# A second feed-forward layer whose down projection is done in the seven-product form

## The chip, the cores and the metric

The kernel runs on one core of a Trainium2 chip. The metric is the device time of one execution in microseconds, from the first to the last instruction with what lies around it. A profiled execution gives a trace as well; times in the trace count from its first instruction.

## The reference

Two layers, each a Fourier mixing and a gated feed-forward, on x of 2048 rows (S) and 640 columns (D); the feed-forward is F = 1728 wide.

```python
def _A_ref(x, dft_seq_re, dft_seq_im, dft_hid_re, dft_hid_im):
    a = jnp.einsum("bsd,ed->bse", x, dft_hid_re)
    b = jnp.einsum("bsd,ed->bse", x, dft_hid_im)
    return jnp.einsum("ts,bse->bte", dft_seq_re, a) - jnp.einsum("ts,bse->bte", dft_seq_im, b)

def _B_ref(x, w_gate, w_up, w_down):
    g = jnp.einsum("bsd,df->bsf", x, w_gate)
    u = jnp.einsum("bsd,df->bsf", x, w_up)
    return jnp.einsum("bsf,fd->bsd", _sigmoid(g) * u, w_down)

for _ in range(2):
    x = x + _A_ref(_layernorm(x), ...)
    x = x + _B_ref(_layernorm(x), B_w_gate, B_w_up, B_w_down)
```

The result is fp32 of the size of x.

## The kernel before

**Numbers.** Each fp32 operand is kept as two fp16 parts, a high part and what it leaves (HI, LO). A product of two such operands takes three matmuls, high by high, high by low and low by high (`PASSES`, line 134). Scales are powers of two (`DS` for w_down, `PH` for the hidden activations).

**Fourier part.** `folded` uses the symmetries of the DFT matrices, so that a quarter of the products is left (`sequence`, `hidden`, lines 773 and 855). That the matrices given have these symmetries, and that the weights lie within the scales, is tested on the chip while the layers run: `load_rows`/`test_rows`, `load_cols`/`test_cols` (lines 1293 to 1319), `load_hidden_rows`, `load_hidden_cols`, `test_w`, `load_edges`. A DFT test loads four pieces of 128 KB through GpSimd's queue (POOL) into one of two rooms, takes differences of mirrored pieces on VectorE (DVE), and adds up their squares on ScalarE (ACT, `square_rest`, line 1277). If the tests fail, the program runs `general` afterwards, a plain version of the whole.

**Feed-forward.** The rows are worked on in four blocks of 512 (`NB`, b = 0 to 3), with the hidden width in tiles of 128: 13 full ones (j = 0 to 12) and a half one, j = 13 (`NF` = 13). Block 0 computes gate and up directly (`gate_up`, line 1051). Blocks 1 to 3 do it by seven products in place of eight for each tile j, in steps of two tiles (`seven`, line 1174, which calls `part_one` to `part_seven`, all through `products`, line 1097). The weights of such a step are G (320 KB), S (512 KB, sums of gate and up weights) and U (192 KB), loaded by `load_s` on SyncE's queue (SP) some steps ahead. The rows of the block, transposed and with their own sums, stand in `XW`, of which there are two, used in turn by `b % 2`; `pair_apply`, `pair_combine`, `pair_parts` make them during the down of the block before, and `pair_transpose` writes them with transposing DMAs (line 516). `up_parts` splits the result h, 512 tokens wide, into two fp16 parts: `ht`, one slot for each j.

**Down.** For each block and each of its four tiles of 128 rows, `down` (line 1235) accumulates over all j in two PSUM banks, one for each half of the 640 columns (`EH` = 320), 82 matmuls (line 1244) in two steps of 42 and 40, and adds the result into X (line 1259); in layer 2 `store_x` writes the rows out at once. The split w_down (`w`, 2, j) lies in a fixed region and is read again from DRAM for layer 2 (`load_w_again`).

**Order.** The kernel writes the order of every engine's queue by hand. `steps` lists TensorE's work; `at(u, f, ...)` puts a piece of other work before step u, and fractions of u order the pieces within a step (a step of `seven` counts two and has four places for pieces, `some(0)` to `some(3)`). So each engine gets its instructions in the order of these places, and each runs its queue in order, waiting on semaphores where data or a slot are not ready. `block[b]` is the first step of block b, `d0` the first of a down.

**Memory.** All tiles lie in `big`, in units of 128 fp32 columns. X, the two `XW` and the split w_down have fixed places; the rest is shared out by `Slots.take` in program order, and a tile that gets a slot waits for the last readers of what was in it. The eight PSUM banks are handed out in the order in which they were freed (`bank`, `free_bank`).

## Time and profile before

| what | value |
|---|---|
| time, median of 3 runs | 1161.23 us (1159.2 to 1161.76) |
| time of the profiled execution | 1158.61 us |
| its span | 1156.8 us |
| granted TensorE clock | 0.999 |
| DMA, mean | 187 GB/s, 216.46 MB |

The page gives each engine's busy time and its share of the span, forty slices of the span with the busy tenths of each engine, and the chain of work that ended last, followed back from the last instruction. PE is TensorE's matmuls, PEld its weight loads. In a row of a group stand line, engine, operation, output and input with shapes and count; then busy time, mean length of one in ns, and the idle time of the engine in front of them with what ended it. In a row of windows stand the stretch and its length, then busy time and count of each engine, the granted clock, the DMA share and GB/s.

### The profile page before, as it was taken

How to read it: one execution, taken by the hardware profiler on the slowest of the kernel's cores; microseconds unless marked ns; L12 is line 12 of the kernel's file. 1: busy time of each engine (PE TensorE's matmuls, PEld its weight loads, DVE VectorE, ACT ScalarE, POOL GpSimd, SP SyncE). 2: the span in 40 equal slices, each digit the busy share in tenths (PEclk: the TensorE clock that was granted, in tenths of full speed). 3: DMA queues.
4: the chain of work that ended last, by engine and by line, in shares of the span. 5: the costliest groups of instructions: out<-in, count | busy, mean ns of one | idle time of the engine just before them, and what ended most of it. 6: DMA issues, size and time to landing. Idle time of an engine off the chain costs nothing.

```text
span 1156.8 us, 22767 instructions
## 1 busy us (share of the span) xinstructions
PE 1127.3 (97%) x8784; PEld 860.0 (74%) x8784; DVE 738.5 (64%) x1636; ACT 507.7 (44%) x1094; POOL 368.4 (32%) x581
## 2 busy tenths in 40 slices
PE   6699999999999999999999999999999999999997
PEld 2467446788878887888776844678887888788875
DVE  7996888768747676585428567666974457524540
ACT  6864575155525653365304322325552455225420
POOL 2312675223545454421000023453355223221000
PEclk9999999999999999999999999999999999999999
DMA  8417698967495959878103562698649881996301
GB/s 267 148 46 236 241 355 281 259 209 212 144 265 182 252 179 194 264 191 258 47 18 110 190 200 73 129 264 262 222 142 258 247 270 56 199 240 184 132 19 38
DMA packets 158693, 216.46 MB, mean 187 GB/s; under 512 B 70194, under 2 KB 103883, under 8 KB 158574
## 3 DMA queue, kind: packets, MB, share of 16 engines
q1 hardware_dynamic: 140014, 166.97, 49.8%
q0 software_dynamic: 18560, 47.93, 14.1%
q8 instruction: 71, 1.16, 0.4%
q14 instruction: 48, 0.39, 0.1%
HBM read 171.03 MB, written 30.40 MB: 174 GB/s over the span
## 4 chain that ended last, share of the span: by engine, by line
PE 84%; DMA 2%; ACT 1%; POOL 1%; DVE 0%; issue 0%; SPq 0%; DVEq 0%; POOLq 0%
PE acc L1097 40%; PE acc L1244 31%; PE acc L1051 8%; PE acc L855 2%; PE acc L1180 2%; PE acc L773 1%; DMA kept_s<-big 1%; DMA kept_w<-big 1%; ACT big L236 1%; DVE big L238 0%; POOL big L1001 0%; PE acc L523 0%; ACT big L479 0%; ACT big L480 0%; POOL big L999 0%
## 5 line engine op out<-in xcount | busy, mean ns | idle before, releaser
L1097 PE MATMUL acc<-big 128*128 128x256 f16 x4212 | 462.8, 273 | 0.0
L1097 PEld LDWEIGHTS <-big 128*128 128x128 f16 x4212 | 412.1, 98 | 48.2
L1244 PE MATMUL acc<-big 128*128 128x320 f16 x2624 | 357.7, 299 | 0.0
L1244 PEld LDWEIGHTS <-big 128*128 128x128 f16 x2624 | 256.7, 98 | 99.7
L1293 POOL DMA_DIRECT2D big<-in_ct x256 | 175.1, 689 | 232.5 <-DVE big L1302 108.0
L1101 ACT ACTIVATE big<-acc 128x256 f32<-128x256 f32 x312 | 116.1, 381 | 208.9 <-PE acc L1097 207.5
L1051 PE MATMUL acc<-big 128*128 128x512 f16 (+1 forms) x990 | 176.5, 340 | 0.8 <-ACT big L236 0.5
L1051 PEld LDWEIGHTS <-big 128*128 128x128 f16 x990 | 96.5, 98 | 79.8 <-ACT big L236 1.0
L1277 ACT ACTIVATE big<-big 128x768 f32<-128x768 f32 (+8 forms) x104 | 79.4, 764 | 112.5 <-DVE big L1302 80.4
L1165 DVE TENSOR_TENSOR big<-big 128x512 f16<-128x512 f32 x78 | 53.8, 689 | 108.9 <-ACT big L1164 108.9
L1259 DVE SCALAR_TENSOR_TENSOR big<-acc,big 128x320 f32<-128x320 f32 x64 | 28.4, 484 | 91.6 <-PE acc L1244 91.5
L238 DVE SCALAR_TENSOR_TENSOR big<-big 128x640 f16<-128x640 f32 (+6 forms) x81 | 64.4, 833 | 2.9 <-ACT big L236 2.3
L1143 ACT ACTIVATE big<-big 128x512 f32<-128x512 f32 x78 | 47.9, 627 | 41.4 <-DVE big L1134 41.2
L236 ACT ACTIVATE big<-big 128x640 f16<-128x640 f32 (+7 forms) x81 | 50.7, 665 | 16.6 <-POOL big L1001 5.3
L1310 POOL DMA_DIRECT2D big<-in_ct x40 | 27.3, 686 | 94.9 <-ACT big L1277 47.3
L1134 DVE TENSOR_TENSOR big<-big,acc 128x512 f32<-128x512 f32 x78 | 53.1, 681 | 3.3 <-PE acc L1097 3.1
L1164 ACT ACTIVATE big<-big 128x512 f16<-128x512 f32 x78 | 48.8, 626 | 7.1 <-DVE big L1155 6.3
L1153 DVE SCALAR_TENSOR_TENSOR big<-acc,big 128x256 f32<-128x256 f32 x78 | 32.6, 418 | 27.9 <-PE acc L1097 22.4
L1299 DVE TENSOR_TENSOR big<-big 128x256 f32<-128x256 f32 x64 | 26.6, 416 | 36.8 <-DMA big<-in_ct 36.8
L855 PE MATMUL acc<-big 128*128 128x321 f16 (+3 forms) x324 | 48.8, 300 | 1.0 <-DVE big L238 1.0
L1300 DVE TENSOR_TENSOR big<-big 128x256 f32<-128x256 f32 x64 | 26.9, 421 | 30.9 <-DMA big<-in_ct 30.9
L509 ACT ACTIVATE big<-big 128x384 f16<-128x384 f32 (+2 forms) x48 | 28.9, 647 | 37.6 <-DVE big L491 17.9
(186 smaller groups left out, 1055.0 us busy)
## 6 DMA issues: line engine op xcount, KB each, us to landing
big<-kept_w SPq DMA_DIRECT2D x125, 320.0 KB, 6.7
big<-kept_s SPq DMA_DIRECT2D x75, 512.0 KB, 5.5
big<-in_ct POOLq DMA_DIRECT2D x256, 128.0 KB, 4.7
big<-kept_w SPq DMA_DIRECT2D x78, 192.0 KB, 5.5
kept_w<-big SPq DMA_DIRECT2D x41, 320.0 KB, 5.3
big<-in_ct POOLq DMA_DIRECT2D x32, 256.0 KB, 3.9
kept_s<-big SPq DMA_DIRECT2D x13, 512.0 KB, 5.2
big<-in_wg SPq DMA_DIRECT2D x16, 320.0 KB, 3.2
```

Source lines behind the costliest of these rows:

```text
L236: nc.scalar.activation(dh, src, AF.Copy, scale=s)
L238: nc.vector.scalar_tensor_tensor(dl, src, s, dh, op0=OP.mult, op1=OP.subtract)
L855: nc.tensor.matmul(ps[:m, :EC], z[:, at : at + m], w[:, 384 * wp : 384 * wp + EC], start=(d == 0 and zp == HI and wp == HI), stop=(d == ND ...
L1051: nc.tensor.matmul(ps, w[wp][:, d * P : (d + 1) * P], xt[:, xp, :], start=(d == 0 and wp == HI and xp == HI), stop=(d == ND - 1 and wp == LO))
L1097: nc.tensor.matmul(ps, wt, xt, start=start and n == 0, stop=n == len(todo) - 1, skip_group_check=not start)
L1101: nc.scalar.activation(dst, ps, AF.Copy)
L1134: nc.vector.tensor_tensor(v, v, other, op=OP.add)
L1164: nc.scalar.activation(s.parts[HI], v, AF.Copy)
L1165: nc.vector.tensor_tensor(s.parts[LO], v, s.parts[HI], op=OP.subtract)
L1244: nc.tensor.matmul(held["pd", e][0][:, :EH], held["ht", j].parts[hp][:, i * P : (i + 1) * P], held["w", 2, j].parts[wp][:, e * EH : (e + 1 ...
L1277: nc.scalar.activation(v, v, AF.Square, accum_out=new_sum()[:p])
L1293: nc.gpsimd.dma_start(v[:, g], bass.AP(ct.tensor, (r * S + row) * S, [[P, NS], [d * S, 16], [1, P]]))
```

## The change

In layer 2 the down of each block takes tiles 0 to 11 in six pairs (`NP` = 6, `PAIRED`). For a pair p let A11, A21 be the first and second 256 tokens of tile 2p of h, A12, A22 those of tile 2p+1, and B11, B12, B21, B22 the column halves of the two tiles of w_down. Then

```
S1 = A21 + A22    T1 = B12 - B11    P1 = A11 B11   P5 = S1 T1
S2 = S1 - A11     T2 = B22 - T1     P2 = A12 B21   P6 = S2 T2
S3 = A11 - A21    T3 = B22 - B12    P3 = S4 B22    P7 = S3 T3
S4 = A12 - S2     T4 = B21 - T2     P4 = A22 T4
C11 = P1 + P2     C12 = P1 + P6 + P5 + P3
C21 = P1 + P6 + P7 + P4             C22 = P1 + P6 + P7 + P5
```

Each product runs over the six pairs for two tiles of 128 rows (i = 0, 1). Products 1, 6, 7 and 8 share chain a, in which the sum grows and is read after each of them; 5 and 3 share chain b; 2 has c, 4 has d: eight banks. "Product 8" is only the rest, tiles 12 and 13, which also goes along with 2, 3 and 4.

```diff
-DS = 2.0**11
+DS = 2.0**9
-PH = 2.0**-16
+PH = 2.0**-18
+NP = 6
+PAIRED = (), (0, 1, 2, 3)
...
+    def first_parts(p, v):
+        a = both(take(6, "A", p, top=UNITS - 8 * NP), 768)[:, :, :256]
+        f = take(8, "af", p).f32
+        nc.vector.tensor_tensor(f[:, 512:768], v[:, :256], v[:, 256:], op=OP.subtract)
+        nc.scalar.activation(a[:, 0], v[:, :256], AF.Copy)
+        nc.vector.tensor_tensor(a[:, 1], v[:, :256], a[:, 0], op=OP.subtract)
+
+    def second_parts(p, v, w):
+        a, f = both(held["A", p], 768)[:, :, 256:], held["af", p].f32
+        s1, s2, s4 = (f[:, 256 * n : 256 * (n + 1)] for n in (0, 1, 3))
+        nc.scalar.activation(a[:, 0], w, AF.Copy)
+        nc.vector.tensor_tensor(s1, v[:, 256:], w[:, 256:], op=OP.add)
+        nc.vector.tensor_tensor(s2, s1, v[:, :256], op=OP.subtract)
+        nc.vector.tensor_tensor(s4, w[:, :256], s2, op=OP.subtract)
+        nc.vector.tensor_tensor(a[:, 1], w, a[:, 0], op=OP.subtract)
+
+    def sum_parts(p):
+        f, s = held["af", p].f32, both(take(8, "AS", p, top=UNITS), 1024)
+        for c in (slice(0, 512), slice(512, 1024)):
+            nc.scalar.activation(s[:, 0, c], f[:, c], AF.Copy)
+        for c in (slice(0, 512), slice(512, 1024)):
+            nc.vector.tensor_tensor(s[:, 1, c], f[:, c], s[:, 0, c], op=OP.subtract)
+        drop("af", p)
...
+    def make_t(p):
+        v, w = (held["dr", 2 * p + k].f32 for k in range(2))
+        b11, b12, b21, b22 = v[:, :EH], v[:, EH:], w[:, :EH], w[:, EH:]
+        nc.vector.tensor_tensor(b11, b12, b11, op=OP.subtract)
+        nc.vector.tensor_tensor(b12, b22, b12, op=OP.subtract)
+        nc.vector.tensor_tensor(b22, b22, b11, op=OP.subtract)
+        nc.vector.tensor_tensor(b21, b21, b22, op=OP.subtract)
...
+        def mm():
+            for n, i in todo:
+                first = (CHAIN[n], i) not in held
+                if first:
+                    held[CHAIN[n], i] = bank()
...
+                for m, (a, w) in enumerate(mms):
+                    nc.tensor.matmul(held[CHAIN[n], i][0][:, :EH], a, w, start=first and m == 0, stop=m == len(mms) - 1,
+                                     skip_group_check=not first)
...
+        def post():
+            for n, i in todo:
...
+                nc.vector.scalar_tensor_tensor(xe, ps[:, :EH], CB, xe, op0=OP.mult, op1=OP.add)
...
+                    order = [[(n, 0), (n, 1)] for n in (1, 5, 2, 3, 6, 4, 7, 8)]
+                else:
+                    order = [[(n, 0), (n, 1)] for n in (1, 5)] + [[(m, i), (n, i)] for i in range(2) for m, n in ((6, 2), (7, 3), (4, 8))]
+                steps += [down_pairs(b, todo, not first) for todo in order]
...
-                u = block[b] - 8 + 1.2 * i
+                u = block[b] - 8 + (0.4 + 2.2 * i if b - 1 in PAIRED[layer] else 1.2 * i)
...
+                    elif q[0] == 0 and j > 3 and b in PAIRED[layer]:
+                        k = j % 2
+                        for what, v in (("G", u - 2 - 0.5 * k), ("S", u - (0.5 if j == NF - 1 else 1 + 0.5 * k)), ("U", u - k)):
+                            at(v, load_s, j, what)
...
-            u0, u1 = block[0] + 8, block[2] + 14
+            free = (block[0] + 4, block[0] + 13, 10), (block[1] + 1, block[1] + 13, 14), (block[2] + 1, block[2] + 13, 14)
```

What else it moves, in words:

- `gated_parts` and `up_parts` call `first_parts` for an even tile and `second_parts` for an odd one; `sum_parts(p)` follows at the end of the step after. The parts of a pair take 6 + 8 units (`A`, `AS`) where two `ht` took 4 + 4, and 8 more (`af`) while they are made.
- The combinations T1 to T4 are made from the raw w_down once, in layer 1's last down (`load_raw`, `make_t`, `split_t`, `keep_t`, a pair every 1.1 steps), and kept in DRAM. T1 lies where B12 lay in the w_down region (`load_down_again`); T2 and T3, 983 KB each, are loaded in layer 2's block 0 into the place of the second `XW` and stay; T4 is loaded for each block by POOL's queue 2.6 steps into its down, and in block 3 into X's first rows.
- From layer 2's block 0 on there is one `XW` (`place`), so the rows of the next block are written when the last gate product of this one has read it. Their preparation starts 0.4 and 2.6 steps into the down instead of 0 and 1.2, and G, S, U of the next block's tiles 0 to 3 are loaded 4, 3, 1 and 0.5 steps ahead of it instead of 8, 7.9, 4.5 and 3.5.
- G and U share one slot of 8 units. In layer 2's blocks 1 to 3, from tile 4 on, S is loaded 1 to 1.5 steps ahead instead of 2 to 2.5, and U at the start of the step that uses it.
- `store_x` of blocks 0 to 2 comes in the next block's gates (`store_later`).
- Tests: layer 1 takes four more of the DFT tests; in layer 2 the DFT tests stand only in the gates, 10 in block 0 and 14 each in blocks 1 and 2, none in the downs; the test of the gate weights moves from block 0 to block 3 (`test_g`); B12's is done in one piece (`test_others`). The combine, join and add of the Fourier rows q = 2 and q = 3 move to block 0's gates. The last `wh` loads go by POOL's queue instead of SP's.
- The row `fw` of layer 1 is spilled to DRAM and read back.

304 lines of the change are left out of this document (258 added, 46 removed).

## The prediction

> **What bounds the kernel now.** First the page's totals, its slices and its chain.
>
> ```profile
> span 1156.8 us, 22767 instructions
> ...
> PE 1127.3 (97%) x8784; PEld 860.0 (74%) x8784; DVE 738.5 (64%) x1636; ACT 507.7 (44%) x1094; POOL 368.4 (32%) x581
> ...
> PE   6699999999999999999999999999999999999997
> ...
> DVE  7996888768747676585428567666974457524540
> ...
> PE 84%; DMA 2%; ACT 1%; POOL 1%; DVE 0%; issue 0%; SPq 0%; DVEq 0%; POOLq 0%
> ```
>
> From the seventh slice on TensorE is never free, and the chain is its matmuls. Removing matmuls there shortens the end one for one, until something else is late. The same chain in order of time, layer 2's last part:
>
> ```profile
> 730.38 44.55 PE acc L1244 x328
> 774.94 71.39 PE acc L1097 x654
> ...
> 1105.82 44.57 PE acc L1244 x328
> 1150.39 0.02 issue
> 1150.41 0.49 DVE big L1259
> ```
>
> A block's down is 328 matmuls in 44.55 us, and nothing stands between it and the next block's gates. What each layer-2 stage has to spare is in the windows (length; then PE, PEld, DVE, ACT, POOL busy; clock, DMA share):
>
> ```profile
> 563.82:608.37 44.55, 44.55 (x330) 32.09 (x329) 10.77 (x31) 1.70 (x3) 1.26 (x1) 1.00 0.06 19
> 649.18:730.38 81.20, 81.20 (x438) 42.65 (x437) 53.18 (x102) 20.03 (x39) 22.94 (x42) 1.00 0.41 127
> 774.94:855.50 80.56, 80.56 (x740) 72.18 (x739) 63.17 (x148) 43.89 (x101) 39.84 (x67) 1.00 0.68 210
> 855.50:900.05 44.55, 44.55 (x330) 32.12 (x329) 24.61 (x58) 13.44 (x26) 20.48 (x29) 1.00 0.91 248
> 900.05:980.62 80.57, 80.57 (x741) 72.19 (x739) 49.08 (x122) 42.41 (x99) 21.68 (x40) 1.00 0.57 187
> 1025.17:1105.82 80.65, 80.65 (x741) 72.19 (x739) 37.98 (x77) 39.00 (x101) 8.09 (x7) 1.00 0.57 165
> ```
>
> They are layer 1's last down, then block 0's gates, block 1's gates and down, and the gates of blocks 2 and 3. VectorE has 17 to 43 us free in a gate stage; DMA has little left in a down.
>
> **The change part by part.** *Matmuls removed.*
>
> ```profile
> L1097 PE MATMUL acc<-big 128*128 128x256 f16 x4212 | 462.8, 273 | 0.0
> L1244 PE MATMUL acc<-big 128*128 128x320 f16 x2624 | 357.7, 299 | 0.0
> ```
>
> An old down has 4 x 2 x (13 x 3 + 2) = 328 matmuls. The new one has seven products x 2 row tiles x 6 pairs x 3 = 252, and the unpaired tiles 12 and 13 take 4 x 2 x (3 + 2) = 40: 292. Four blocks lose 4 x 36 = 144, each 357.7 / 2624 = 0.136 us at the same 320 columns: **-19.6 us**. A gate matmul is 462.8 / 4212 = 0.110 us; I use both to place things.
>
> *VectorE's added work.* For a pair of tiles the combinations replace two 512-wide subtractions (L1165) by five instructions of 256 columns and three of 512: five 256s and one 512 more. What they cost back to back, the timeline of VectorE shows:
>
> ```profile
> 842.03 0.42 DVE L1299 TENSOR_TENSOR big<-big 128x256 f32<-128x256 f32 x1
> 842.36 0.42 DVE L1300 TENSOR_TENSOR big<-big 128x256 f32<-128x256 f32 x1
> 842.82 0.49 DVE L1302 TENSOR_TENSOR big<-big 128x128 f32<-128x128 f32 x2
> 843.23 0.68 DVE L1165 TENSOR_TENSOR big<-big 128x512 f16<-128x512 f32 x1
> 843.83 0.81 DVE L229 TENSOR_REDUCE wmax<-big 128x1 f32<-128x640 f16 x1
> 844.56 0.41 DVE L1133 TENSOR_TENSOR big<-big 128x256 f32<-128x256 f32 x1
> ```
>
> Start to start, 256 columns take 0.33 us, 512 take 0.60, a weight test 0.73, one DFT test 1.20. So a pair adds 5 x 0.33 + 0.60 = 2.25, a block 13.5; by the full lengths (0.42, 0.68) it is 2.8 and 16.7, and I take the first, since in a full queue the next instruction starts before the last has ended. Block 1 also loses the ten combine, join and add instructions of q=3 to block 0, some 6 us by width, and keeps about the same number of DFT tests: 63.2 + 13.5 - 6 = 71 of 80.6. Block 0 gets those of q=2 and q=3 (12), four DFT tests more (4.8) and 13 weight tests fewer (-9.5): 53.2 + 13.5 + 12 + 4.8 - 9.5 = 74 of 81.2. Blocks 2 and 3 come to about 65 and 61. All fit. ScalarE gets one 256 and one 512 more a pair, at most 0.381 + 0.626 = 1.0 us by these rows, 6 a block, on 44 at most of 80.6:
>
> ```profile
> L1101 ACT ACTIVATE big<-acc 128x256 f32<-128x256 f32 x312 | 116.1, 381 | 208.9 <-PE acc L1097 207.5
> ...
> L1164 ACT ACTIVATE big<-big 128x512 f16<-128x512 f32 x78 | 48.8, 626 | 7.1 <-DVE big L1155 6.3
> ```
>
> [...]
>
> *How late VectorE runs.* Adding up what each step of two tiles gives it (10.6 us usual in 11.7 us of PE; row statistics of the next block add 2.1 each at steps 8 and 10, and a third test falls into step 8), VectorE ends step 10 of block 1 five to six us behind. The chain banks that a step writes are freed by the `up` of the step before, some 6 us ahead of need: 0 us if that sum holds, 2 if it is short by two. I take 0.5. In the down VectorE then stands before `pair_combine` of the second half, whose slot the first half's transposes still read. Behind it wait the reads of products 2 and 3; product 5's read, which product 3 needs, is ahead of it.
>
> *Loads with less lead.* The paired tiles hold 14 units each, so weight slots get tight: `load_s` now waits for a slot that `up_parts` or `up` of the step before has just left. Example: S of tile 5. Its slot is free 0.2 us into the step, and its first use (part_six) stands 45 matmuls in, 45 x 0.110 = 5.0: lead 4.8. Going so through the changed kernel's order, these have under 7 us: block 1, S5 4.8, S7 5.3, G11 5.0, G12 5.3; block 2, S5 4.8, S7 5.3, G9 6.2, G11 6.2, G12 4.9; block 3, S5 6.2, S9 4.7, S11 4.7, S12 6.8. Landing times of S (L1024), of single 320 KB loads (L978) and of G with S and U right behind it (L1022):
>
> ```profile
> L1024 SPq DMA_DIRECT2D big<-kept_s x75: 319/383/2047, 222.7 to 1083.3; - x75
> ...
> DMA to landing us min/median/max: 4.0/5.5/14.8
> ```
>
> ```profile
> L978 SPq DMA_DIRECT2D big<-kept_w x47: 319/382/1166, 279.0 to 1086.0; - x47
> ...
> DMA to landing us min/median/max: 3.8/5.2/6.9
> ```
>
> ```profile
> L1022 SPq DMA_DIRECT2D big<-kept_w x78: 319/544/2126, 215.1 to 1082.9; - x78
> ...
> DMA to landing us min/median/max: 3.2/8.0/13.3
> ```
>
> At the shortest landings nothing waits: 0. At 5.5 for S and 5.2 for G, which now goes out alone as in L978, the shortfalls are 0.7 + 0.2 + 0.2, then 0.7 + 0.2 + 0.3, then 0.8 + 0.8: **+3.9**, which I take. At 8.0 for all thirteen they sum to 34. SP's queue is in order: while an S waits for its slot, U of the same step and the next G stand behind it; U has over 8 us.
>
> *One place for the rows (XW).* The transposes now wait for the block's last gate product and are issued later; behind them on SP's queue stand G, S and U of the next block's first tiles, formerly ahead.
>
> ```profile
> 865.66 6.10 SPq L516 DMA_TRANSPOSE big<-big  x2
> ...
> 875.72 6.95 SPq L516 DMA_TRANSPOSE big<-big  x2
> 882.72 1.57 SPq L1022 DMA_DIRECT2D big<-kept_w  x1
> ```
>
> Now the second pair is issued 20.2 us after the down's start. In the changed kernel the first pair goes out at 13.5 (VectorE is late), its slot is released by about 21, the second pair is ready at 25 and through SP at 32; G lands at 37 to 40, and the down lasts 292 x 0.136 = 39.8. 0 to 3 us at the starts of blocks 2 and 3; block 1's, where VectorE is not late, is safe. I take 0.5 each: +1. T4 (983 KB through POOL) has a lead of 13.7 us in a full DMA stage: 0 to 2 each in blocks 1 and 2, I take 0.5 in all.
>
> *Chain a.* Product 8 of row tile 1 overwrites what L1259's successor must first read; product 8 of tile 0 (5 x 0.136 = 0.68) covers its 0.48:
>
> ```profile
> L1259 DVE SCALAR_TENSOR_TENSOR big<-acc,big 128x320 f32<-128x320 f32 x64 | 28.4, 484 | 91.6 <-PE acc L1244 91.5
> ```
>
> 0 to 0.4 a block; 0.1 each, +0.4. Twice as many such reads (16 a block) lie in downs that have lost their tests.
>
> *At nothing:* the combinations of W2 in layer 1's last down, 24 subtractions of 320 columns and 12 low parts of 640, by the spacings above about 0.40 and 0.73 each, 18 us of VectorE, and 12 high parts, some 9 of ScalarE; the first window covers them (10.8 and 1.7 busy of 44.55, DMA 0.06). Without that cover the first folds after the down would be late. T2 and T3, loaded once, go into block 0's gates (DMA 0.41). Stores move from downs into gates (0.91 to 0.57). Four tests more in layer 1, the spilled row, the last wh loads on POOL's queue: each a few us on engines with room.
>
> **Sum:** -19.6 + 0.5 + 3.9 + 1 + 0.5 + 0.4 = -13.3. The profiled execution took 1158.61 (span 1156.8), so 1145.3; its time stands 2.6 below the median of the runs, 1161.23, which becomes **1148**.
>
> **The rivals.** *Nothing waits.* All terms but the first vanish: 1161.2 - 19.6 = 1141.6. For it: shortest landings. Against: thirteen loads below 7 us of lead. 14%.
>
> *The weight loads set the pace (slower).* Place: the slots of S and G, blocks 1 to 3. At 8.0 us a load the waits are 34 in place of 3.9: 1178. It turns the change into a loss where the landings average above some 6.7 us (17 us of waits). For it: L1022's median, DMA share 0.68 in block 1's gates, stores added there. Against: the 8.0 is of trains of 1 MB. 8%.
>
> *VectorE becomes the bound.* Its waits in block 1's gates:
>
> ```profile
> DVE big L1165 <- ACT big L1164: 8.4, 8, 2.1
> DVE big L1300 <- DMA big<-in_ct: 5.9, 4, 4.3
> ```
>
> If the three splits of a pair each wait 1.05 (8.4 / 8) for ScalarE, 18.9 a block, and these waits stay, block 1 needs 71 + 3 + 18.9 + 14.3 = 107, 27 too many, 21 after the 6 that are free; block 2, in the same way, 14, block 3 some 5: +40, 1187. Against: when VectorE is late, ScalarE is ahead of it. [...] 7%. That the program's own test falls over the changed scale (DS) and the general path runs: 1%.
>
> **How the numbers follow.** Forecast 70%, its own range 1143 to 1157. 0.2% is 2.3 us, about what a measurement of this kernel can tell from no change: faster ends at 1158.9. Faster: 0.68 + 0.14 = 0.82; the forecast's upper end and milder forms of the two slow rivals give 0.05 for same; slower 0.13. The range takes in the free case and stretches up to where the loads eat the gain: 1141 to 1162.
>
> **What would show it.** The down group at 292 matmuls a block in layer 2 and 39.8 us long; gaps in TensorE only in front of S and G products, most in block 1, none in block 0, each below 2 us; VectorE about 71 us busy in block 1's gates. It is wrong if TensorE idles over 8 us in all, if it waits for VectorE's reads of PSUM, or if a down starts late.

## The result, and the profile after

| what | before | after |
|---|---|---|
| time, median of 4 runs each | 1161.49 us (1159.2 to 1165.15) | 1193.18 us (1186.93 to 1197.6) |
| profiled execution, its span | 1158.61 us, 1156.8 | 1197.6 us, 1195.8 |
| granted TensorE clock | 0.999 | 0.986 |

The ratio is 1.0265, with an interval of 1.023 to 1.03: slower by 32 us, where 13 us less were forecast. The traced execution of the changed kernel is the slowest of its four, so stages read from the traces differ by 39 us in all (the spans). The page of the changed kernel has these totals, slices (forty of some 30 us; the clock in tenths), shares of the chain, and the groups of the gates' and the downs' matmuls:

```profile
span 1195.8 us, 22910 instructions
...
PE 1119.2 (94%) x8640; PEld 847.9 (71%) x8640; DVE 829.9 (69%) x1849; ACT 531.9 (44%) x1154; POOL 378.7 (32%) x594
...
PE   5699989999999999999999999998899999849997
...
L1177 PE MATMUL acc<-big 128*128 128x256 f16 x4212 | 473.7, 275 | 37.5 <-ACT big L1181 17.8
...
L1460 PE MATMUL acc<-big 128*128 128x320 f16 x1168 | 159.9, 299 | 5.2 <-DVE big L1477 3.7
```

The 144 matmuls are gone (8784 to 8640) and TensorE is busy 8 us less, yet the gates' products (L1177, formerly L1097) stood still for 37.5 us in front of them, where it was 0.0. The same 4212 products also took 473.7 us in place of 462.8. Of these 10.9 us, some 8 come from products run at a granted clock of 0.50 (the last section shows the stretches); the rest stands at full clock in stages that are interrupted often (block 1's gates: 83.33 busy, less some 1.5 for their stretch at 0.50, against 80.56 before). The chain of waits in order of time shows layer 2's block 0 as it was meant (gates, then down):

```profile
661.39 81.20 PE acc L1122 x435
742.59 39.73 PE acc L1460 x292
```

Where the time is lost, the windows show by stage (length; then busy time of PE, PEld, DVE, ACT, POOL; clock, DMA share, GB/s). First before's gates of layer 1's block 2, then of the changed kernel the same gates, block 1's gates and down, block 2's gates, its down with the gap behind it, block 3's gates and down:

```profile
348.46:429.02 80.56, 80.56 (x740) 72.22 (x738) 58.59 (x150) 45.46 (x107) 40.39 (x75) 1.00 0.72 204
```

```profile
352.34:441.17 88.83, 82.88 (x741) 73.05 (x738) 61.42 (x159) 47.30 (x111) 46.72 (x83) 0.98 0.72 215
782.15:874.43 92.28, 83.33 (x741) 72.64 (x738) 71.07 (x177) 46.36 (x113) 40.27 (x66) 0.98 0.66 202
874.43:914.15 39.72, 39.72 (x294) 28.57 (x292) 23.10 (x46) 9.20 (x16) 6.09 (x9) 1.00 0.65 150
914.15:1003.29 89.14, 83.24 (x740) 72.80 (x738) 65.01 (x164) 46.55 (x113) 29.81 (x48) 0.98 0.65 218
1003.29:1058.29 55.00, 40.31 (x294) 28.45 (x292) 24.46 (x49) 11.80 (x24) 10.14 (x10) 0.95 0.73 104
1058.29:1148.58 90.29, 83.91 (x739) 73.43 (x739) 61.12 (x125) 42.09 (x111) 12.15 (x14) 0.94 0.65 194
1148.58:1188.40 39.82, 39.82 (x294) 28.47 (x291) 13.78 (x40) 3.66 (x6) 3.45 (x5) 1.00 0.14 52
```

Three downs take 39.7 to 39.8 in place of 44.55, as summed. Against that stand +8.3 in layer 1's block 2 (88.83 against 80.56), +11.7 in block 1's gates, +8.6 in block 2's, +10.4 in block 2's down and the gap behind it (55.00 against 44.55), +9.6 in block 3's gates. Layer 1's first gate-up and its block 1 add 4 (85.2 against 82.3, 81.7 against 80.6 by their windows). In these five windows TensorE is idle for 41.9 us (length less busy time). What it waits for from 640 us on (total, times, longest; the three largest of five):

```profile
PE acc L1177 <- DMA big<-kept_w: 16.4, 5, 9.5
PE acc L1177 <- ACT big L1181: 11.8, 6, 3.3
PE acc L1460 <- DVE big L1477: 3.7, 2, 2.4
```

Weights (`kept_w`) come first, then ScalarE's copies out of PSUM (L1181). The timeline of block 1's gates shows how the second kind arises (start, length, engine, line; in brackets the idle time before and what ended it):

```profile
819.73 0.43 DVE L1566 TENSOR_TENSOR big<-big 128x256 f32<-128x256 f32 x1 [2.65 <-DMA big<-in_ct]
820.19 0.50 DVE L1568 TENSOR_TENSOR big<-big 128x128 f32<-128x128 f32 x2
...
820.77 0.85 ACT L1543 ACTIVATE big<-big 128x768 f32<-128x768 f32 x1 [4.96 <-DVE big L1568]
...
822.65 0.63 ACT L1181 ACTIVATE big<-acc 128x256 f32<-128x256 f32 x2
...
823.07 0.82 PE L1177 MATMUL acc<-big 128*128 128x256 f16 x6 [1.61 <-ACT big L1181]
```

VectorE stands 2.65 us before a DFT test whose data (`in_ct`) have not landed. ScalarE stands 4.96 before that test's square (L1543), because it needs VectorE's difference (L1568). Behind the square in ScalarE's queue stand the copies that free TensorE's banks, with a split (L1355) in between, so TensorE stands too. Each of the three engines has stood idle in turn, and none of them is short of time.

The start of block 3 is the other loss. The timeline of the second half of block 2's down:

```profile
1013.87 31.32 SPq L547 DMA_TRANSPOSE big<-big  x4
...
1032.35 0.56 DVE L529 TENSOR_TENSOR big<-big 128x384 f32<-128x384 f32 x1 [12.56 <-DMA big<-big]
...
1039.83 5.05 PE L1460 MATMUL acc<-big 128*128 128x320 f16 x36 [1.29 <-DVE big L1477]
1045.25 0.57 SPq L1066 DMA_DIRECT2D big<-kept_w  x1
...
1047.30 1.52 PE L1460 MATMUL acc<-big 128*128 128x320 f16 x10 [2.42 <-DVE big L1477]
...
1058.29 1.46 PE L1177 MATMUL acc<-big 128*128 128x256 f16 x6 [9.47 <-DMA big<-kept_w]
```

SP's queue is held for 31.32 us by four transposes, the last two of which wait for rows that VectorE makes late. VectorE waits 12.56 us at L529, in the making of the second pair's rows (`pf`), until the first pair's transposes have read what lies at their address. The reads of PSUM (L1477) stand behind it, so the down itself stops. The weights of block 3's first tile (L1066) leave at 1045.25, and their landing ends a gap of 9.47. The trace times the landing of only the last transpose of a group. In layer 2 of this kernel that is one of twelve, the last ahead of block 3, issued at 1040.7:

```profile
DMA to landing us min/median/max: 16.5/16.5/16.5
```

Before, two were timed in layer 2, at 5.9 and 8.7 us. That the first pair was slow as well shows in L529, which could start only 18.5 us after that pair's first transpose was issued.

### The profile page after: what moved, and what is told of

Read it like the earlier page. It is cut to its first block, busy times and chain, and to the rows that moved or that the text cites. A ratio compares the mean times of both kernels' runs of the same rounds, so it can differ in the third digit from the quotient of the medians.

```text
span 1195.8 us, 22910 instructions
## 1 busy us (share of the span) xinstructions
PE 1119.2 (94%) x8640; PEld 847.9 (71%) x8640; DVE 829.9 (69%) x1849; ACT 531.9 (44%) x1154; POOL 378.7 (32%) x594
## 4 chain that ended last, share of the span: by engine, by line
PE 54%; DMA 12%; DVE 9%; ACT 3%; issue 3%; SPq 1%; POOL 1%; ACTq 0%; DVEq 0%; POOLq 0%
PE acc L1177 27%; PE acc L1510 7%; PE acc L1122 7%; PE acc L1460 7%; DMA big<-kept_w 4%; DMA big<-in_ct 4%; DMA big<-big 2%; PE acc L896 2%; PE acc L1269 2%; PE acc L814 1%; ACT big L1543 1%; DVE big L541 1%; POOL big L1559 1%; DVE big L1214 1%; SPq L547 1%
## 5 line engine op out<-in xcount | busy, mean ns | idle before, releaser
L1177 PE MATMUL acc<-big 128*128 128x256 f16 x4212 | 473.7, 275 | 37.5 <-ACT big L1181 17.8
L1177 PEld LDWEIGHTS <-big 128*128 128x128 f16 x4212 | 414.8, 99 | 94.1 <-issue 19.8
L1181 ACT ACTIVATE big<-acc 128x256 f32<-128x256 f32 x312 | 113.2, 379 | 198.6 <-PE acc L1177 194.6
L1510 PE MATMUL acc<-big 128*128 128x320 f16 x1312 | 178.9, 299 | 0.0
L1460 PE MATMUL acc<-big 128*128 128x320 f16 x1168 | 159.9, 299 | 5.2 <-DVE big L1477 3.7
L1510 PEld LDWEIGHTS <-big 128*128 128x128 f16 x1312 | 128.4, 98 | 49.8
L1122 PEld LDWEIGHTS <-big 128*128 128x128 f16 x990 | 96.3, 98 | 82.9 <-ACT big L254 3.6
L1460 PEld LDWEIGHTS <-big 128*128 128x128 f16 x1168 | 114.2, 98 | 50.2 <-issue 5.8
L1543 ACT ACTIVATE big<-big 128x768 f32<-128x768 f32 (+8 forms) x104 | 79.6, 765 | 151.2 <-DVE big L1568 92.8
L254 ACT ACTIVATE big<-big 128x640 f16<-128x640 f32 (+7 forms) x93 | 59.5, 675 | 44.3 <-DVE big L1373 18.9
L256 DVE SCALAR_TENSOR_TENSOR big<-big 128x640 f16<-128x640 f32 (+6 forms) x93 | 74.0, 828 | 7.1 <-ACT big L254 5.0
L1254 DVE TENSOR_TENSOR big<-big 128x512 f16<-128x512 f32 x42 | 28.9, 688 | 48.9 <-ACT big L1253 48.7
L1477 DVE SCALAR_TENSOR_TENSOR big<-acc,big 128x320 f32<-128x320 f32 x64 | 29.5, 486 | 43.2 <-PE acc L1460 43.0
L1213 DVE TENSOR_TENSOR big<-big 128x256 f32<-128x256 f32 x78 | 32.6, 418 | 15.3 <-ACT big L1181 15.1
```

What stands on the lines that cost most here:

```text
L254: nc.scalar.activation(dh, src, AF.Copy, scale=s)
L256: nc.vector.scalar_tensor_tensor(dl, src, s, dh, op0=OP.mult, op1=OP.subtract)
L1122: nc.tensor.matmul(ps, w[wp][:, d * P : (d + 1) * P], xt[:, xp, :], start=(d == 0 and wp == HI and xp == HI), stop=(d == ND - 1 and wp == LO))
L1177: nc.tensor.matmul(ps, wt, xt, start=start and n == 0, stop=n == len(todo) - 1, skip_group_check=not start)
L1181: nc.scalar.activation(dst, ps, AF.Copy)
L1460: nc.tensor.matmul(held[CHAIN[n], i][0][:, :EH], a, w, start=first and m == 0, stop=m == len(mms) - 1, skip_group_check=not first)
```

## The experiments

In all of them "rows apart" is the second edit below, which most later ones contain. Stages are given as lengths of windows; 80.56 is a seven-product gate stage that nothing holds up. Each length comes from one traced execution, and the same work in the same order came out differently: in five kernels that share the tests of layer 2's blocks 0 to 2, block 1's gates took 89.56 to 94.91 us and block 2's 86.50 to 89.80; layer 1's block 2 took 85.24 to 90.51 in seven kernels with the same layer 1. Only what lies outside these ranges counts as an effect on them.

| kernel | median, us | ratio to before, interval |
|---|---|---|
| changed kernel | 1193.18 | 1.0265 (1.023 to 1.03) |
| tests as before | 1179.35 | 1.0156 (1.0128 to 1.0185) |
| rows apart | 1174.81 | 1.0125 (1.0108 to 1.0142) |
| rows apart, tests as before | 1183.19 | 1.0182 (1.0136 to 1.0229) |
| rows apart, no tests in layer 2 | 1151.17 | 0.992 (0.9894 to 0.9946) |
| rows apart, hidden-matrix tests late | 1178.36 | 1.0137 (1.0109 to 1.0166) |
| rows apart, layer 1's tests later | 1173.65 | 1.0132 (1.0059 to 1.0204) |
| rows apart, only block 0 paired | 1186.14 | 1.022 (1.0191 to 1.025) |
| rows apart, test loads out in layer 2 | 1164.34 | 1.0016 (0.9992 to 1.0041) |
| rows apart, test work out in layer 2 | 1182.94 | 1.0185 (1.0143 to 1.0226) |
| rows apart, squares out | 1165.38 | 1.0039 (1.0007 to 1.007) |
| third, fourth, fifth spread of tests | 1179.63, 1174.06, 1164.44 | 1.016, 1.0124, 1.0039 |
| first down alone | 1161.39 | 0.9997 (0.9977 to 1.0016) |
| first down alone, reloads spread | 1159.07 | 0.9991 (0.9975 to 1.0006) |

### The tests as before

```diff
-            free = (block[1] + 5, block[3] + 13, 46),
+            free = (block[1] + 6, block[3] + 13, 42),
...
-            free = (block[0] + 4, block[0] + 13, 10), (block[1] + 1, block[1] + 13, 14), (block[2] + 1, block[2] + 13, 14)
+            free = (block[0] + 8, block[2] + 14, 42),
...
-        tests = tests[0] + tests[1][:4] if first else tests[1][4:]
+        tests = tests[layer]
```

> Both layers' DFT tests and the wh tests stand where the kernel before had them (42 a layer; layer 2's from block 0's middle to block 2's end, so that some fall into the downs); all else is the changed kernel. Theory 1 (the tests' new spread makes VectorE and ScalarE late): layer 1 loses its 12 us again, the gates of blocks 1 and 2 come down from 92.4 and 89.3 to about 82, and only the stall round block 3's start (some 25 us) stays: about 1193 - 12 - 10 - 7 = 1164. Rival (VectorE's new combinations alone are too much for the gate stages): layer 1 comes back, the gates of blocks 1 and 2 stay near 90: about 1181.

It came out 13.8 us below the changed kernel, about half of what was expected. Layer 1's gates are whole again (80.6), block 2's nearly (82.15), but block 1's take 89.28, and the tests that now stand in the downs of blocks 1 and 2 make those 45.90 and 46.93 long: TensorE waits there for VectorE's reads of PSUM (4.8 and 4.1 us). So the number and places of the tests explain layer 1 and block 2. Block 0's down, with six or seven tests in it, keeps its 39.73: a short down can hold tests, and what else makes the later two late is not told apart here.

For layer 1 alone, its 42 tests went back and the four others into block 3's gates:

```diff
+            free = (block[1] + 6, block[3] + 13, 42),
...
+            free = (block[0] + 4, block[0] + 13, 10), (block[1] + 1, block[1] + 13, 14), (block[2] + 1, block[2] + 13, 14), (block[3] + 1, block[3] + 13, 4)
```

> Only layer 1's tests stand as before (42 of them, pace 1.167 steps in place of 1.087); the four that were moved to layer 1 are put into block 3's gates; the windows of blocks 0 to 2 in layer 2 keep their 38. Theory 1: the gates of layer 1's block 2 go back from 89.0 to 81 and those of block 1 from 81.9 to 81; 1193 - 9 to 12 = 1181 to 1184, with the gates of layer 2's blocks 1 and 2 still at 89 to 92. Rival (layer 1's loss is not the four tests but a chance state of the DMA queues in that run): the loss stays or moves, 1190 to 1195.

Those four came to share the two rooms with the tests of the hidden matrices, whose loads wrote over their data, so `general` ran as well: 4277.66 us. Its layer 1 can still be read: 80.56, 80.56 and 80.6 for the three gate stages of blocks 1 to 3, the second of which took 88.83 in the changed kernel.

### The rows of the second pair at another address

```diff
-        v = take(19, "pf", b, i).f32
+        v = take(19, "pf", b, i, top=(239, 275)[i] if one and b > 1 else 0).f32
...
-        h, l = (held["pb", b, i] if n else take(NT, "pb", b, i)).parts
+        h, l = (held["pb", b, i] if n else take(NT, "pb", b, i, top=(256, 292)[i] if one and b > 1 else 0)).parts
```

> Same instructions in the same order on every engine; only the addresses of the second pair's rows at the starts of blocks 2 and 3 differ, so that they don't lie on what the first pair's transposes still read. Theory 2 (that wait on VectorE, 8.0 and 12.6 us, holds the second transposes back, and behind them on SP's queue the next block's first weights): VectorE's wait for the transposes is under 2 us, the third down is back at 39.9 us from 45.5, block 3's gates start on time in place of 9.5 us late, and their 90.5 us become 84 to 86: 1193 - 20 = about 1173. Rival (the weights stand behind four transposes on SP in any case, and those alone take too long): the down is whole again, but block 3 still starts over 5 us late: about 1185.

Nothing but the addresses of the two pairs' rows in blocks 2 and 3 differs, and 18.4 us are gone, in sum as expected. The windows of layer 1's block 2 gates, then of layer 2 from block 1's gates to block 3's (block 1's down left out), and its waits of TensorE from 640 us on:

```profile
350.01:436.76 86.75, 82.65 (x740) 73.05 (x738) 61.42 (x159) 47.74 (x111) 47.84 (x85) 0.98 0.76 225
777.74:867.30 89.56, 81.72 (x740) 71.87 (x738) 70.99 (x177) 46.52 (x113) 40.48 (x66) 1.00 0.66 205
...
907.03:993.53 86.50, 81.31 (x740) 72.03 (x738) 64.18 (x163) 46.64 (x113) 29.84 (x48) 1.00 0.64 215
993.53:1033.80 40.27, 39.89 (x295) 28.47 (x292) 25.53 (x50) 11.90 (x24) 10.52 (x10) 1.00 0.90 147
1033.80:1125.00 91.20, 83.56 (x738) 73.31 (x739) 61.05 (x125) 42.11 (x110) 12.09 (x14) 0.96 0.66 193
```

```profile
PE acc L1177 <- ACT big L1181: 9.1, 5, 2.5
PE acc L1177 <- DMA big<-kept_w: 6.7, 3, 6.1
PE acc L1177 <- DMA big<-kept_s: 4.4, 4, 1.6
```

Block 2's down is on time (40.27 with its gap, from 55.00). That the slots overlapped is shown as the cause of 14.7 us there: in the changed kernel VectorE's L529 waited 8.0 and 12.6 us for transposes, here for none. The rest of the gain is gates that came out 2 to 3 us shorter, which is within their range. Block 3's gates, expected at 84 to 86, are not shorter: they still wait 6.1 us once for weights, with the DMA engines at 0.90 in the down before it.

Both edits together were to tell whether they add up:

> Both edits together. Theories 1 and 2: the two gains add up, 1193 - 29 - 20 = about 1144, below the kernel before (some 1161) by the saved matmuls less a few us. If the combinations on VectorE bound the gate stages: blocks 1 and 2 still at 89 to 92, 1161 or above.

They don't: 1183.19. Block 1's down is 48.80, 7.7 us of it one wait for L1477, and block 2's down with its gap 59.28, 19.4 of it one wait for `kept_w`. In these two downs VectorE's reads come late, and behind them the rows of the next block, their transposes (the last landed after 22.6 us), and the weights that SP issues behind these.

### What of a test costs

The 38 DFT tests and 14 hidden-matrix tests of layer 2 left out, on rows apart:

```diff
+        if not first:
+            free, tests = (), [None]
...
-            tests = [(load_hidden_rows, test_hidden_rows, (r, k), 14.5 + 1.4 * (4 * r + k), 2.4) for r in range(2)
...
+            tests = ()
```

> On top of the rows kept apart (1174.8 us), layer 2's 38 DFT tests and 14 wh tests are left out (their loads, VectorE and ScalarE work); combinations and weight loads stay. Theory A (tests and combinations together are more than VectorE and ScalarE can do in a gate stage; each alone fits): the gates of blocks 1, 2 and 3 come to 81 to 83 from 89.6, 86.5 and 91.2; only waits for weight slots of 1 to 3 us a block stay: about 1174.8 - 20 = 1155. Theory B (the combinations' chain alone makes the gates late, or the weight loads do): they stay above 86, 1165 or more.

1151.17, faster than before by 0.8%. The gates of blocks 1, 2 and 3, and the landing of the last transpose ahead of block 3:

```profile
776.45:857.01 80.56, 80.56 (x740) 72.21 (x738) 55.76 (x123) 37.63 (x87) 8.02 (x18) 1.00 0.43 139
896.74:977.30 80.56, 80.56 (x740) 72.21 (x738) 46.53 (x108) 37.39 (x87) 8.00 (x18) 1.00 0.43 139
1017.03:1097.60 80.57, 80.57 (x741) 72.21 (x739) 51.87 (x109) 37.17 (x87) 2.04 (x2) 1.00 0.44 138
```

```profile
DMA to landing us min/median/max: 5.3/5.3/5.3
```

From 640 us on TensorE does not wait once. The weights' short lead suffices, with the combinations and the single `XW` in place; everything that rows apart still loses in layer 2 needs the tests. Which half of a test it is, two kernels ask. One leaves out the test loads of layer 2 and keeps all work on them (the rooms are zeroed once); the other keeps the loads and leaves out the work:

```diff
-                at(u, load, *key)
+                if first:
+                    at(u, load, *key)
...
-                at(block[2] + u, load, *key)
```

> On top of the rows kept apart (1174.8 us): in layer 2 the loads of the 38 DFT and 14 wh tests are left out and their two rooms are zeroed once; the tests' VectorE and ScalarE instructions all stay where they are. Theory E (the gathers do it: VectorE waits in its order for data that land late, and the gathers slow the weight loads; the vector work itself fits): gates of blocks 1 to 3 at 81 to 82, block 3 on time, as without tests: about 1152. Theory F (71, 64 and 61 us of VectorE work in 80.6, with ScalarE in turns, is too much whatever the data do): gates stay at 86 or more, only block 3's start is mended: about 1168.

```diff
-                at(u + (1 if first else 1.4) * pace, test, *key)
-                at(u + (1.7 if first else 1.8) * pace, square_rest)
+                if first:
+                    at(u + pace, test, *key)
+                    at(u + 1.7 * pace, square_rest)
...
-                at(block[2] + u + later, test, *key)
-                at(block[2] + u + 1.15 * later, square_rest)
```

> On top of the rows kept apart: in layer 2 the same loads of the 38 DFT and 14 wh tests run, but the tests' VectorE and ScalarE instructions are left out. If the gathers' share of the DMA engines alone makes the weights late: TensorE's waits for kept_s and kept_w stay (11 us in that kernel, 6 of them at block 3's start), gates 83 to 86 and block 3 late, about 1163; its waits for the copies out of PSUM (13 us) fall to layer 1's 4. If it takes the tests' instructions too (late VectorE, late slots, late loads): waits for weights under 3 us, about 1153.

Without the loads, blocks 1 and 3:

```profile
783.39:872.45 89.06, 83.06 (x741) 72.91 (x739) 71.84 (x179) 46.55 (x113) 7.30 (x18) 0.98 0.40 126
...
1038.29:1120.47 82.18, 80.90 (x741) 72.12 (x739) 61.41 (x126) 42.60 (x111) 3.36 (x2) 1.00 0.43 136
```

Block 1 keeps its whole loss (89.06 against 89.56), with the DMA engines at 0.40, and block 2 too (86.39 against 86.50). There it is the work on VectorE and ScalarE, not the loads. So the wait for data that have not landed, with which the timeline above begins, is not what makes these two late: here VectorE never waits for test data, and yet ScalarE's squares in block 1 wait for VectorE:

```profile
ACT big L1543 <- DVE big L1568: 16.7, 8, 3.4
```

Block 3 is nearly whole (82.18 against 91.20), and the last transpose lands after 5.0 us: there it is the loads. The other kernel agrees for blocks 2 and 3 (81.80, and 90.34 with 49.87 for the down before it, its last transpose landing after 22.9), but block 1 loses 9 us in it as well (89.95, of it 4.1 waiting for `kept_w`). In this kernel no work on the data holds the next loads back, so this run says less.

If the loads of the hidden-matrix tests in block 2's down are what delays block 3, putting them into block 3's gates should help:

```diff
-            tests = [(load_hidden_rows, test_hidden_rows, (r, k), 14.5 + 1.4 * (4 * r + k), 2.4) for r in range(2)
+            tests = [(load_hidden_rows, test_hidden_rows, (r, k), 23.5 + 0.85 * (4 * r + k), 1.45) for r in range(2)
```

> On top of the rows kept apart, the 14 wh tests start at block 3's second step in place of 14.5 steps into block 2, so their gathers leave block 2's down. Theory C (in that down the four transposes, T4's load, the wh gathers and the next block's first weights share the DMA engines, busy share 1.05 to 1.35 from 1010 to 1045 us, so that the second weight tile of block 3 lands late): TensorE's 6.1 us wait at block 3's start falls under 2 us and block 3's gates to 84 to 86: 1174.8 - 6 = about 1168. Rival (the transposes and the weights alone fill it): the wait stays over 4 us, 1173 to 1176, or more where the wh tests now make VectorE late in block 3.

Block 3 started on time, and its gates took 90.64 all the same, with 14 tests in them. Its blocks 1 and 2, at 94.91 and 89.80, are the long ends of the ranges above, so the total (1178.36) doesn't tell whether the move alone cost or gained; block 3's gates it did not mend.

### Layer 1, and ScalarE's squares

On rows apart, layer 1's tests stand 1.4 intervals behind their loads in place of 1, the squares 1.8 in place of 1.7:

```diff
-                at(u + (1 if first else 1.4) * pace, test, *key)
-                at(u + (1.7 if first else 1.8) * pace, square_rest)
+                at(u + 1.4 * pace, test, *key)
+                at(u + 1.8 * pace, square_rest)
```

> On top of the rows kept apart, layer 1's 46 tests stand 1.4 paces behind their loads in place of 1.0 (square at 1.8 in place of 1.7); the number of tests and VectorE's work are the same. Theory D (in layer 1 VectorE waits in its order for the gathers of tests that come too close behind their loads): VectorE's waits for in_ct in the gates of layer 1's block 2 fall from 13 us to under 3, and those gates from 86.7 to 81: 1174.8 - 6 = about 1169. Rival (46 tests are too many for VectorE there): no change, 1173 to 1176, or worse because the rooms come free later.

The same gates of layer 1's block 2 take 82.14 in place of 86.75. VectorE's waits there, rows apart first and then this kernel, agree:

```profile
DVE big L1566 <- DMA big<-in_ct: 6.8, 6, 1.4
DVE big L1565 <- DMA big<-in_ct: 5.6, 3, 3.3
```

```profile
DVE big L1565 <- DMA big<-in_ct: 2.6, 1, 2.6
DVE big L1566 <- DMA big<-in_ct: 0.8, 1, 0.8
```

The whole time did not follow (1173.65 against 1174.81). In the trace, layer 1 ends some 6 us earlier, and layer 2 gives most of it back without an edit there: 91.43 and 88.88 in the gates of blocks 1 and 2 (89.56 and 86.50 on rows apart) and 41.81 in block 2's down (40.27). Layer 1's first gate-up varies as well, from 82.0 to 86.8 us across the kernels of this study, tied to no edit.

ScalarE's part was asked by leaving out the squares of the tests. The edit took them out of both layers, not of layer 2 alone as the expectation has it:

```diff
     def square_rest():
-        square_sum(rest.pop(0))
+        v = rest.pop(0)
+        if not first:
+            return
+        square_sum(v)
```

> On top of the rows kept apart (1174.8 us): in layer 2 the squares and sums of the 52 tests on ScalarE are left out (a test's loads and VectorE work stay). Theory G (ScalarE, in its order, stands at a square that waits for a late VectorE test while the copies out of PSUM stand behind it): TensorE's waits for those copies fall from 13 us to layer 1's 4 to 5, the gates of blocks 1 and 2 go from 89.6 and 86.5 to 82 to 84: about 1164. Rival H (VectorE is late by its own work; the copies wait for it through the chain of a step, squares or not): blocks 1 and 2 stay at 86 or more, 1171 to 1176.

The gates of layer 1's block 2 and of layer 2's blocks 1 and 2:

```profile
351.81:432.38 80.57, 80.57 (x741) 72.21 (x739) 59.90 (x155) 38.20 (x85) 45.20 (x82) 1.00 0.79 224
773.34:861.93 88.59, 83.67 (x741) 72.47 (x739) 67.93 (x169) 36.03 (x85) 39.43 (x64) 0.98 0.66 201
902.47:985.47 83.00, 81.27 (x741) 71.88 (x738) 61.39 (x156) 36.22 (x86) 28.43 (x47) 1.00 0.70 234
```

Layer 1's block 2 is whole with the tests at the changed kernel's distance (its block 1 took 82.54), and layer 2's block 2 gains 3.5. TensorE's waits for ScalarE's copies from 640 us on fall from 9.1 to 1.7 us. ScalarE was never short of time (36 to 48 busy of 80.6); the order in its queue was. Block 1 stays at 88.6, where TensorE now waits mostly for weights (3.4 of its 4.9 us) and runs for a time at a lower clock (0.66 on the mean from 815 to 820).

Whether the combinations matter to block 1, a kernel asks in which only block 0 is paired. In blocks 1 to 3 T1 then stands in place of half of w_down, and some of their parts lie on its tiles, so only block 1's gates are read. The edit also gives the weights of block 1's tiles from 4 on their old, longer lead:

```diff
-PAIRED = (), (0, 1, 2, 3)
+PAIRED = (), (0,)
```

> On top of the rows kept apart, only block 0's down has the seven-product form; blocks 1 to 3 have the old downs and no combinations, but the changed kernel's tests, one place for the rows, and resident tiles. Theory A: without the combinations the same tests fit, the gates of blocks 1 and 2 come to 81 to 82 and block 3's start is not late: 1161 - 4.8 (one down) + 6 (layer 1) = about 1162. Theory B' (the tests' pace alone makes the gates late): blocks 1 and 2 stay at 86 to 90, about 1175.

86.55 with VectorE 57.00 busy, against 89.56 (up to 94.91) with 70.99. So leaving out the combinations, with the longer lead, gains 3 us there or more, and leaving out the tests gains everything (80.56 with the combinations in place). Before, block 1's gates held 12 tests without loss. Neither is too much alone; the two do not simply add up.

### Other spreads of the tests

Fifty tests in layer 1 and 34 in layer 2, five of them in block 3's gates, and the hidden-matrix tests behind them:

```diff
+            free = tuple((block[b] + u0, block[b] + u1, n) for b, u0, u1, n in ((0, 4, 13, 10), (1, 1, 13, 9), (2, 1, 13, 10), (3, 1, 5, 5)))
```

> All work done, rows kept apart, tests spread anew: 50 in layer 1 at the same pace as now (from its block 1's second step on) and 1.4 paces behind their loads; in layer 2 10, 9, 10 and 5 in the gates of blocks 0 to 3, the wh tests in block 3's gates after them. If the tests' pace in the gates of blocks 1 and 2 (one in 5.3 us) is what makes them late, one in 8 us as here lets them run at 81 to 83, layer 1's block 2 at 81 to 82, block 3 on time with a few us lost in its gates: about 1152 to 1158. If the combinations leave no room for any tests: 1165 or more.

The loads of the hidden-matrix tests wrote over the last test's data, and `general` ran too (4286.73 us), so the total says nothing. The gates ahead of that can be read: block 2's took 81.79 with 10 tests, but block 1's 92.52 with 9, where TensorE waited 9.5 us for weights and not once for ScalarE. So one test in 8 us is no cure for block 1 by itself. The next kernels take more tests into layer 1, fewer into blocks 1 and 2, with a fixed distance between load and test:

```diff
-            free = (block[1] + 5, block[3] + 13, 46),
+            free = (block[1] + 1, d0 + 5, 56),
...
+            free = (block[0] + 4, block[0] + 13.5, 10), (block[1] + 1, block[1] + 13, 8), (block[2] + 1, block[2] + 13, 10)
```

> All work done, rows kept apart. 56 tests in layer 1 (from block 1's second step to the middle of its last down, pace 1.11 steps, 1.4 paces behind their loads), 10, 8 and 10 in the gates of layer 2's blocks 0 to 2, tested 1.2 steps after the load, the wh tests in block 3's gates at 1.2 steps. If the number of tests in a gate stage decides: blocks 1 and 2 at 83 to 85, block 3 on time and 84 to 86 long, layer 1 at 81 to 83 a stage: 1155 to 1160. If any test in block 1's gates is too many, or the tests in layer 1's last down make layer 2's opening late: 1165 or more.

Blocks 1 and 2, with 8 and 10 tests, took 82.9 and 81.5. But layer 1's last down, which now holds tests, took 8.0 us longer with the Fourier products behind it (85.76 against 77.75 in the changed kernel), and the second pair's parts lay on tiles of w_down still in use, so its later stages do not count. Then 54 tests in layer 1's gates alone, 12, 8 and 10 in layer 2's, the rows at whatever place the transposes do not read:

```diff
+            free = (block[1] + 1, block[3] + 13, 54),
...
+            free = (block[0] + 4, block[0] + 13.5, 12), (block[1] + 1, block[1] + 13, 8), (block[2] + 1, block[2] + 13, 10)
...
+                at(u + (1.4 * pace if first else 1.2), test, *key)
+                at(u + min(1.95 * pace, 2.4), square_rest)
```

> All work done; the pairs' rows apart in both blocks by a first fit that spares what the transposes still read. 54 tests in layer 1's gates and downs from block 1's second step (pace 1.0 step, 1.4 paces behind the load), none in its last down; 12, 8 and 10 in the gates of layer 2's blocks 0 to 2, tested 1.2 steps after the load; each square as late as its room allows; the wh tests within block 3's gates. From the runs so far: layer 1 loses 1 to 4 us, blocks 1 and 2 come to 82 to 83 (spread3 had 82.9 and 81.5), block 3 starts on time and takes 84 to 87, downs at 39.7: 1161 - 19.6 + 3 + 4 + 6 = about 1154, 1150 to 1158. If the wh tests or layer 1's closer tests cost as much as the old places: 1162 or more.

It came to 1174.06, above the 1150 to 1158 expected. The gates of layer 1's block 1 and of layer 2's block 1, and the hidden-matrix tests' block 3:

```profile
226.84:314.73 87.89, 81.22 (x740) 72.12 (x738) 63.88 (x164) 44.25 (x111) 39.16 (x71) 1.00 0.72 216
...
794.00:875.53 81.53, 80.90 (x740) 72.04 (x738) 63.96 (x154) 42.99 (x101) 24.69 (x42) 1.00 0.61 190
...
1037.15:1124.51 87.36, 81.75 (x740) 71.78 (x738) 62.70 (x126) 44.44 (x115) 19.77 (x20) 1.00 0.72 201
```

The first two rows have the same VectorE load (63.88 and 63.96) and differ by 6.4 us. Not the sum sets the time; among what differs is the number of tests, some 13 against 8. Block 0's down, behind 12 tests in its gates, took 47.97 in this kernel, 8.2 us too long. The last spread has 50 in layer 1 and 10, 10 and 14 in layer 2:

```diff
+            free = (block[1] + 5, block[3] + 13, 50),
...
+            free = (block[0] + 4, block[0] + 13, 10), (block[1] + 1, block[1] + 13, 10), (block[2] + 1, block[2] + 13, 14)
```

> All work done, as spread4, but 50 tests in layer 1 from block 1's sixth step on (pace 1.0), and 10, 10 and 14 in the gates of layer 2's blocks 0 to 2; the rows apart and the wh tests as in spread4. From spread4's stages: layer 1's block 1 back at 81 from 87.9, block 0's down back at 39.7 from 48.0, blocks 1 and 2 at 83 to 85, block 3 as there at 87: 1174 - 7 - 8 + 3 = about 1162, 1156 to 1166. If squares placed later and fewer tests in block 1 matter less than thought, blocks 1 and 2 go back to 87 to 90 and it is 1168 or more.

1164.44: all downs 39.7 to 39.9, and 85.62, 86.76 and 88.81 in the gates of blocks 1 to 3, which give back what the downs gain. Ten tests in a gate stage came out at 81.5 and 82.2 us in block 2 and at 85.6 in block 1 in these three kernels: their number alone does not set the time either.

### Only the first down

Block 0 was the one block of the changed kernel without loss, so the last two kernels change its down alone and keep the tests and two `XW` as before; B12 is reloaded over T1 afterwards, in the first of them in the opening of block 1's gates, in the second one tile at a time later (the last edit line shown is the second's):

```diff
-PAIRED = (), (0, 1, 2, 3)
+PAIRED = (), (0,)
...
-        return 0 if one else b % 2
+        return (b + len(one)) % 2
...
+                for p in range(NP):
+                    at(block[0] + 28 + 1.2 * p, load_first_again, p)
```

> All work done. Only block 0's down of layer 2 has the seven-product form (its combinations fall into block 0's gates, where nothing was late in any run); blocks 1 to 3 have the old down and the two places for their rows; the tests stand as in the kernel before; the halves of W2 that T1 displaces are loaded again after that down (six loads of 160 KB). If the gain of one down (36 matmuls, 4.8 us) is kept where VectorE's load of the other gates is as before: 1160 - 4.8 + 0 to 2 = 1155 to 1157. If the start of block 1 (transposes and first weights in a shorter down, with tests in it) gives it back: 1160 or more, block 1's gates over 83 us.

> As first_down, but the six loads that bring back W2's halves go out one by one from the seventh step of block 1's gates on, in place of in one row at their start (9.1 us on SP's queue, ahead of the gates' weights, 776 to 785 us), and the loads for the test of these halves stand in block 2. If that row of loads is what took the gain back (block 1's gates 85.6 us in place of 80.6): gates at 81 to 82, 1161.4 - 4 = about 1157 to 1158, ratio 0.996 to 0.997. If the shorter down before them or the gathers in it delay the weights: gates stay over 84, 1160 to 1162.

Neither is told apart from the kernel before. In the first, six reloads in a row hold SP's queue for 9.1 us ahead of weights, and block 1's gates take 85.55. In the second the down takes 40.18 and the gates lose 2.9 (83.43, DMA share 0.85), so that 1.5 of the 4.4 us gained are left. No kernel of this study that does all the work beats the one before by more than a measurement can tell.

## Why the prediction was wrong, point by point

**Matmuls removed: right.** -19.6 was forecast. Three downs came to 39.73, 39.72 and 39.82 in place of 44.55, 44.55 and 44.57, 4.8 each, so 19.2 for four. Chain a shows no cost in them; T4 came late once, by 1.5 us (0.5 in the sum).

**VectorE's busy time: right; "All fit": wrong, and the largest error.** Blocks 1, 2 and 3 came to 71.07, 65.01 and 61.12 against the 71, 65 and 61 worked out, block 0 to 71 against 74. The step from there, that a stage with 9.5 to 19 us to spare fits, is the one that failed. The sum asked how much each engine does, not in which order two in-order engines wait for each other. A test ties POOL's load, VectorE's difference and ScalarE's square into a chain, and the square stands ahead of PSUM copies; in block 1's gates of the changed kernel the squares waited eight times, 20.2 us in all, for VectorE, and TensorE three times, 7.2 us, for the copies. Leaving out the tests freed blocks 1 and 2 wholly (80.56). Leaving out their loads alone did not, so in these two it is the work in its order, not late data. Leaving out the squares freed layer 1's block 2 wholly and layer 2's block 2 by 3.5, leaving out the combinations freed block 1 by 3 or more. The term of 0.5 for VectorE's lateness in block 1 stood for what measured +11.7 there and +8.6 in block 2. For block 2 the square's place is thus shown as part of the cause. For block 1 it is shown only that it takes the tests' work: the 8 us that remain without squares are 4.9 of waits, 3.4 of them for weights, and 3.1 of longer products, and why the weights are late there stays open.

**"At nothing", four tests more in layer 1: wrong.** They had no profile row of their own in the prediction. They cost 8.3 us in block 2's gates (4.7 to 10 in the seven kernels), as 46 tests at the shorter interval find their data not landed; a distance of 1.4 intervals brings the stage to 82.1, the old 42 tests to 80.6. The rest of that list (the combinations of w_down, T2 and T3, the stores) cost nothing that shows: layer 1's last down and block 0 kept their lengths.

**Loads with less lead: about right in size here, for another reason.** 3.9 was forecast; without the 14.9 at block 3's start (two waits of 9.5 and 5.4), TensorE waited 3.9 for weights in the gates of the changed kernel and some 5 on rows apart (4.4 for S, 0.6 for G). That it is so close is luck: block 1 alone waited 1.7 in the changed kernel and 9.5 in the second spread. Without tests the waits are 0, so thirteen short leads alone cost nothing. The slow rival built on them is refuted: its 34 us came in no kernel.

**One place for the rows: the mechanism was named, the size was not.** The step took the first pair's slot as "released by about 21" and allowed 0 to 3 us a block. In block 2's down it was 29 (L529 at 1032.35, the down from 1003.29), as the first pair, out at 10.6 and not at 13.5, was read only 18.5 us after its issue, where the step allowed some 7.5, and its transposes read the very units into which the second pair is written. That cost 14.7 in the down and gap (shown by moving the address alone). The 6.1 that then stays goes with the loads (82.18 without them).

**The clock was not in the sum at all.** Of the 10.9 us by which the gate products grew, some 8 come from four stretches at a granted clock of 0.50, each behind idle time of TensorE (last section).

**The rivals.** "VectorE becomes the bound" came nearest in number (1187 against 1193), by luck, and in place, the tests' waits for data among its terms. Its main term, splits that each wait for ScalarE, was not what happened: ScalarE waited for VectorE and TensorE for ScalarE. The 3 us that its 107 adds to the 71 no run shows: VectorE's busy time in block 1's gates came to 71.07. A test it would have needed, whether the time follows VectorE's sum, came out no (63.88 and 63.96 busy, 87.89 and 81.53 long).

**The signs** named for being wrong: TensorE idled over 8 us, and waited for VectorE's reads of PSUM (3.7). No down started late; what did, by 9.5 us, was block 3's gates.

Open: why layer 1's first gate-up and the gates of the same program vary by several us, and the cause of block 1's rest. Not tried: a third room for the test data, and the squares on another engine.

## What to carry to other kernels

A free share of an in-order engine says nothing of whether work fits into it: list, for each piece that is put in, what it waits for and what stands behind it, on every engine it passes through, and give it the distance that its load's landing needs (in layer 1 that alone brought a stage from 86.75 to 82.14). When two buffers become one or slots grow, look up which addresses the allocator reuses, for a reuse adds a wait that the source does not show. And count a stall by more than its length: here some 16 us of products behind four stalls ran at a granted clock of 0.50, which cost some 8 us on top of the stalls.
